# Moving the pooled v product to the head of three FFN slots, and the transposes onto other banks first

## The chip, the cores and the metric

The kernel runs on one core of a Trainium2 chip. The metric is the device time of one execution in microseconds, median of several runs. The TensorE clock in the page of the profile was granted in full for nearly the whole span.

Engines are called as the profile calls them: PE is TensorE, PEld its weight loads, ACT is ScalarE, DVE is VectorE, POOL is GpSimd.

## The reference

```python
# q, k, v: (8, 8, 576, 64); factor 4; scale = 1/8
q_d, k_d, v_d = mean over 4 neighbouring positions of q, k, v        # 144 positions
out_up    = repeat(softmax(scale * q_d @ k_d.T) @ v_d, 4)            # pooled attention
out_local = softmax(scale * q @ k.T where |i - j| < 4) @ v           # band attention
x   = (out_up + out_local) as 4608 tokens x 512
out = (relu(x @ w_gate) * (x @ w_val)) @ w_out                       # 512 -> 1536 -> 512
```

## The kernel before

The attention is worked off in 32 head pairs, `hp`. Four are done first (`emit_fill`); after that the program goes through "slots". Slot `s` holds a quarter of the FFN work of one chunk of 512 tokens, and between its parts the attention work of head pair `s + 4`, so that PE always has matmuls. Everything is scheduled by hand: on each engine the instructions run in the order in which the program emits them.

PSUM is one tile of eight banks, and `pair(i)` is banks 2i and 2i+1. The parts that matter, in slots 1 to 3:

| name in this text | line before / after | what it is | banks |
|---|---|---|---|
| denominators | L363, L372 / L367, L376 | column sums of the exponentials of the last head pair | 4, 5 |
| numerators | L382, L391 / L386, L395 | v times the exponentials | 2, 3 |
| projections | L483 / L487 | 4 matmuls for gate, 4 for value; three such pairs a slot | 0-1, 2-3, 6-7 |
| scores | L279, L290 / L283, L294 | q by k of this head pair | 4 to 7 |
| pooled v | L263 / L267 | 6 matmuls that sum v over 4 positions, and an ACT copy | 5, then 1 |
| transposes | L226 / L228 | q and k of the next head pair, 24 matmuls | 4, 0, 1 |

```python
def emit_qkT_pe(hp, b0, b1):
    ...                                         # cut
    blocks = list(range(2 * NB))                # 12 blocks, 4 to a bank
    if hp == 0:
        blocks = blocks[NB:] + blocks[:NB]
    for n in blocks:
        lo = 120 * (n % 4)
        bank = b0 if n < 4 else b1 + n // 4 - 1
        for hh in range(2):
            nc.tensor.matmul(out=ps[64 * hh : 64 * hh + 64, bank, lo : lo + 120],
                lhsT=sv[:, n // NB, hh, n % NB, :], rhs=eyesum_sb, start=True, stop=True)
    ...                                         # cut: views of the outputs
    act, dve = nc.scalar.copy, nc.vector.tensor_copy
    ...                                         # cut: the plan for hp == 0
    plan = ((0, 1, act), (0, 0, act), (1, 1, dve), (2, 1, dve), (2, 0, dve), (1, 0, act))
    for i, pooled, copy in plan:                # (bank index, pooled part?, engine)
        ...                                     # cut: copy of a bank's pooled or full part

def emit_vd(hp, bank):                          # pooled v
    t = vw[hp % NL][:, :, 0:64].rearrange("p (h j) d -> p j h d", h=2)
    o = ps[:, bank, 0:256].rearrange("p (c h d) -> p c h d", c=2, h=2)
    for c in range(2):
        for sig in range(3):
            nc.tensor.matmul(out=o[:, c, :, :], lhsT=pool_sb[0:WK, sig, :],
                rhs=t[:, 3 * c + sig, :, :], start=(sig == 0), stop=(sig == 2))
    nc.scalar.copy(out=vd[hp % 3].rearrange("p c (x d) -> p c x d", x=3)[:, :, 0:3:2, :], in_=o[0:72])

def emit_s2t(hp, between):
    ...                                         # cut: denominators into banks 4, 5
    ...                                         # cut: numerators into banks 2, 3
    r, x = rden[r2], xn[r2]
    nc.scalar.activation(out=r, in_=ps[:, 4:6, 0:360], func=AF.Ln)
    between()                                   # the gate of the previous projections
    nc.scalar.activation(out=r, in_=r, func=AF.Exp, scale=-1.0)
    nc.vector.tensor_tensor(out=x, in0=ps[:, 2:4, 0:360], in1=r, op=ALU.mult)
    emit_xsum(hp)

def emit_h(c, jj, pp, parts=...):               # projections into pair(pp)
    ...                                         # cut: the matmuls
    def gate():
        nc.scalar.activation(out=r1, in_=h1, func=AF.Relu)
        nc.vector.tensor_tensor(out=gt, in0=r1, in1=h2, op=ALU.mult)
    return gate

def emit_slot(s, gate):
    ...                                         # cut: loads, and slot 0
    if s <= 5:
        if s == 5:
            emit_pool(hp)
        emit_s2t(hp - 1, gate)
    ...                                         # cut: slots over 4
    if s == 4:
        emit_y(c - 1, s % 4, 1)
    else:
        emit_h(c, jj, 0)()
    emit_s1(hp, 4)                              # scores
    if s == 4:
        emit_h(c, jj, 0)()
    emit_h(c, jj + 1, 1)()
    emit_vd(hp, 5)
    if hp + 1 < NTP:
        emit_qkT_pe(hp + 1, 4, 0)
    return emit_h(c, jj + 2, 3)                 # its gate runs inside the next slot's emit_s2t
```

The softmax here doesn't subtract the row's maximum and nothing guards it: scores larger than these inputs give would overflow.

Of the kernel before, what the change touches and what calls it, by code (L numbers as in the profile page):

```python
# [57 lines left out]
def kernel(  # L58
# [25 lines left out]
    NTP = 9  # L84
# [122 lines left out]
    def emit_pool(hp):  # L207
        with nc.allow_low_precision(reason="4:1 pooling sum"):
            nc.vector.tensor_reduce(
                out=qkd[hp % 2].rearrange("p i t -> p (i t)"),  # L210
                in_=qkT[hp % 4][:, 0 : 2 * S].rearrange("p (t f) -> p t f", f=4),
                axis=AX.X,
                op=ALU.add,
            )

    def emit_qkT_pe(hp, b0, b1):
        r, r4, r2 = hp % NL, hp % 4, hp % 2
        sv = qk16[r].rearrange("p i (h j d) -> p i h j d", h=2, d=64)
        blocks = list(range(2 * NB))
        if hp == 0:  # L220
            blocks = blocks[NB:] + blocks[:NB]
        for n in blocks:
            lo = 120 * (n % 4)
            bank = b0 if n < 4 else b1 + n // 4 - 1
            for hh in range(2):
                nc.tensor.matmul(  # L226
                    out=ps[64 * hh : 64 * hh + 64, bank, lo : lo + 120],
                    lhsT=sv[:, n // NB, hh, n % NB, :],  # L228
                    rhs=eyesum_sb,
                    start=True,  # L230
                    stop=True,
                )
        big = qkT[r4][:, 0 : 2 * S].rearrange("p (b n t) -> p b n t", b=3, n=4)
        sml = qkd[r2].rearrange("p i t -> p (i t)").rearrange("p (b n t) -> p b n t", b=3, n=4)
        act, dve = nc.scalar.copy, nc.vector.tensor_copy
        if hp == 0:
            plan = ((2, 1, act), (2, 0, act), (1, 1, dve), (1, 0, dve), (0, 1, act), (0, 0, dve))
        else:
            plan = ((0, 1, act), (0, 0, act), (1, 1, dve), (2, 1, dve), (2, 0, dve), (1, 0, act))
        for i, pooled, copy in plan:  # L240
            bank = b0 if i == 0 else b1 + i - 1
            t = ps[:, bank, 0:480].rearrange("p (n t) -> p n t", n=4)
            if pooled:
                copy(out=sml[:, i], in_=t[:, :, 96:120])
            else:
                copy(out=big[:, i], in_=t[:, :, 0:96])

    def emit_vd_pool(hp):
        t, m, o = v4[hp % NV4], v2[hp % 2], vd[hp % 3]
        nc.gpsimd.tensor_tensor(out=m, in0=t[:, :, 0:128], in1=t[:, :, 128:256], op=ALU.add)  # L250
        nc.gpsimd.tensor_tensor(  # L251
            out=o.rearrange("p c (x d) -> p x c d", x=3)[:, 0:3:2, :, :],
            in0=m[:, :, 0:64].rearrange("p (h c) d -> p h c d", h=2),
            in1=m[:, :, 64:128].rearrange("p (h c) d -> p h c d", h=2),
            op=ALU.add,
        )

    def emit_vd(hp, bank):
# [4 lines that stand above are left out]
                nc.tensor.matmul(  # L263
                    out=o[:, c, :, :],
                    lhsT=pool_sb[0:WK, sig, :],
                    rhs=t[:, 3 * c + sig, :, :],
                    start=(sig == 0),  # L267
                    stop=(sig == 2),
                )
        nc.scalar.copy(  # L270
            out=vd[hp % 3].rearrange("p c (x d) -> p c x d", x=3)[:, :, 0:3:2, :], in_=o[0:72]
        )
# [85 lines left out]
    def emit_s2t(hp, between):  # L358
        r2 = hp % 2
        e, d = ee[r2], ed[r2]  # L360
        for g in range(2):
            for hh in range(2):
                nc.tensor.matmul(  # L363
                    out=ps[64 * hh : 64 * hh + 64, 4 + g, 0:288],
                    lhsT=ones_sb[0:WK, 0:64],
                    rhs=e[:, hh, 288 * g : 288 * g + 288],
                    start=True,  # L367
                    stop=True,
                )
            for c in range(2):  # L370
                for hh in range(2):
                    nc.tensor.matmul(  # L372
                        out=ps[64 * hh : 64 * hh + 64, 4 + g, 288:360],
                        lhsT=ones_sb[0:72, 64:128],
                        rhs=d[:, hh, c * SD + 72 * g : c * SD + 72 * g + 72],
                        start=(c == 0),  # L376
                        stop=(c == 1),
                    )
        for g in range(2):
            for j in range(3):  # L380
                for hh in range(2):
                    nc.tensor.matmul(  # L382
                        out=ps[64 * hh : 64 * hh + 64, 2 + g, NQ * j : NQ * j + NQ],
                        lhsT=vw[hp % NL][:, NB * hh + 3 * g + j, 0:64],
                        rhs=e[:, hh, 288 * g + NQ * j : 288 * g + NQ * j + NQ],
                        start=True,  # L386
                        stop=True,
                    )
            for c in range(2):
                for hh in range(2):  # L390
                    nc.tensor.matmul(  # L391
                        out=ps[64 * hh : 64 * hh + 64, 2 + g, 288:360],
                        lhsT=vd[hp % 3][:, c, 128 * hh : 128 * hh + 64],
                        rhs=d[:, hh, c * SD + 72 * g : c * SD + 72 * g + 72],
                        start=(c == 0),  # L395
                        stop=(c == 1),
                    )
        r, x = rden[r2], xn[r2]
        nc.scalar.activation(out=r, in_=ps[:, 4:6, 0:360], func=AF.Ln)  # L399
        between()  # L400
# [4 lines that stand above are left out]
    def emit_xsum(hp):  # L405
        b, kk, x = hp // NPB, hp % NPB, xn[hp % 2]
        nc.vector.tensor_tensor(  # L407
            out=xT[:, kk, b * S : (b + 1) * S].rearrange("p (c t f) -> p c t f", c=2, f=4),
            in0=x[:, :, 0:288].rearrange("p c (t f) -> p c t f", f=4),
            in1=_sap(x, (0, 128), 288, [[360, 2], [1, 72], [0, 4]]),  # L410
            op=ALU.add,
        )
# [184 lines left out]
    def emit_slot(s, gate):  # L597
        c, jj, hp = s // 4, 3 * (s % 4), s + LEAD
        if NVP <= hp + 1 < NP:
            emit_vd_pool(hp + 1)  # L600
        emit_in(hp + 4)
        if NTP <= hp + 3 < NP:
            emit_qkT(hp + 3)
        if s == 0:
            emit_qkT_pe(hp, 2, 3)
            emit_h_mm(c, jj, 3, 1, range(3))
            emit_h_mm(c, jj, 3, 0, range(1))
            emit_x_pe(hp - 1, 0)
            emit_h(c, jj, 3, ((0, range(1, 4)), (1, range(3, 4))))()
            emit_s1(hp, 2)  # L610
            emit_h(c, jj + 1, 0)()
            emit_vd(hp, 6)
            emit_qkT_pe(hp + 1, 2, 3)
            return emit_h(c, jj + 2, 3)
        if s <= 5:
            if s == 5:
                emit_pool(hp)
            emit_s2t(hp - 1, gate)
        elif gate:
            gate()  # L620
        if s > 4:
            if hp < NP:
                emit_y(c - 1, s % 4, 1 if s == 5 else 2, 6 if s == 5 else 2, lambda: emit_s1(hp, 4))
            else:
                emit_y(c - 1, s % 4, 2)
            if hp < NVP:
                emit_vd(hp, 3)
            if hp + 1 < NP:
                emit_pool(hp + 1)
            emit_h(c, jj, 0)()  # L630
            if hp < NP:
                emit_s2w(hp)
            emit_h(c, jj + 1, 1)()
            gate = emit_h(c, jj + 2, 0)
            if hp < NP:
                gate()
                emit_xsum(hp)
                return None
# [5 lines that stand above are left out]
        emit_s1(hp, 4)  # L644
        if s == 4:
            emit_h(c, jj, 0)()
        emit_h(c, jj + 1, 1)()
        emit_vd(hp, 5)
        if hp + 1 < NTP:
            emit_qkT_pe(hp + 1, 4, 0)  # L650
        return emit_h(c, jj + 2, 3)

    with tc.manual_schedule(engines={ET.PE, ET.DVE, ET.Activation, ET.SP, ET.Pool}):
# [49 lines left out]
```

## Time and profile before

| | before |
|---|---|
| time, median of the first 3 runs | 357.59 us (357.54 to 358.28) |
| span of the profiled run | 356.6 us |
| PE busy | 97% of the span |
| slots 1, 2 and 3 on PE | 8.29 us each |
| PE wait inside each of them | 0.26 us |

The first lines are from the page of the kernel before: the busy time of each engine, and the shares of the chain of work that ended last.

```profile
PE 347.2 (97%) x2851; PEld 177.8 (50%) x2851; DVE 227.0 (64%) x344; ACT 211.5 (59%) x358; POOL 189.0 (53%) x233
...
PE 90%; DVE 4%; ACT 3%; DMA 1%; issue 1%; DVEq 0%; POOLq 0%
```

The kernel is bound by PE. Time can only come from fewer matmuls or from the few places where PE stands still. Those are in the list of waits of PE (waiting line, what it waited for, total us, times, longest); these three lines lie in slots 1 to 3 and in slot 5:

```profile
PE ps L424 <- DVE ee_103 L302: 0.7, 1, 0.7
...
PE ps L483 <- DVE xn_114 L402: 0.5, 2, 0.3
PE ps L483 <- DVE xn_115 L402: 0.3, 1, 0.3
```

Next is slot 1 on PE, from the timeline (start, duration, what; several equal matmuls on one line; in brackets the idle time before and what ended it). A duration reaches to the end of the last result, so it overlaps the next line's start: read start to start.

```profile
31.90 1.03 PE L483 MATMUL ps<-xT,wv_sb 128*128 128x512 f16 x4
32.86 0.31 PE L363 MATMUL ps<-ee_102,ones_sb 112*64 112x288 f16 x2
...
34.63 1.03 PE L483 MATMUL ps<-xT,wv_sb 128*128 128x512 f16 x4
35.59 0.26 PE L279 MATMUL ps<-qkd_101 64*72 64x144 f16 x2
...
36.42 1.02 PE L483 MATMUL ps<-xT,wg_sb 128*128 128x512 f16 x4 [0.26 <-DVE xn_114 L402]
37.28 1.03 PE L483 MATMUL ps<-xT,wv_sb 128*128 128x512 f16 x4
38.14 0.50 PE L263 MATMUL ps<-vw_94,cst_sb 112*128 112x128 f16 x6
38.57 0.82 PE L226 MATMUL ps<-cst_sb,qk_6_81 96*64 96x120 f16 x24
...
41.15 0.31 PE L363 MATMUL ps<-ee_103,ones_sb 112*64 112x288 f16 x2
```

From 32.86 to 41.15 are 8.29 us. Only one line has a bracket. Pooled v at 38.14 starts as soon as the value projections let it (four matmuls of 0.216 us after 37.28), and has no wait. Six matmuls of 0.056 us end at about 38.48; the transposes start 0.09 us later, and the same gap stands before the denominators and before the scores, with no bracket.

The wait at 36.42 ends a chain on ACT and DVE. Here are ACT's lines from its timeline:

```profile
33.47 0.77 ACT L399 ACTIVATE rden_112<-ps 128x720 f32<-128x720 f32 x1 [1.70 <-PE ps L372]
34.14 0.59 ACT L498 ACTIVATE r_752<-ps 128x512 f16<-128x512 f32 x1
34.62 0.81 ACT L401 ACTIVATE rden_112<-rden_112 128x720 f32<-128x720 f32 x1
```

And DVE's line that PE waits for:

```profile
35.46 0.91 DVE L402 TENSOR_TENSOR xn_114<-ps,rden_112 128x720 f16<-128x720 f32 x1
```

The denominators end, then come the logarithm, the gate relu of the previous projections, the exponential, and the product, which reads banks 2 and 3. The second projections want to write those banks.

### The profile page before, as it was taken

What the parts mean: (1) busy time and instruction counts of PE and PEld (TensorE: products, weight loads), DVE (VectorE), ACT (ScalarE), POOL (GpSimd) and SP (SyncE); (2) the same over time, 40 slices, a digit from 0 to 9 for tenths busy, and PEclk for the clock granted to TensorE, in tenths of its full rate; (3) what the DMA queues carried; (4) which work ended last, traced back from release to release, by engine and by line L of the source; (5) the groups of instructions that cost most, each with busy time, mean ns of one, the idle gap of its engine ahead of it and who ended that gap; (6) DMA issues with size and microseconds to landing.
All of it is one profiled execution on the core that took longest, in us unless ns stands there. A gap on an engine that the chain in (4) does not pass through costs nothing.

```text
span 356.6 us, 7224 instructions
## 1 busy us (share of the span) xinstructions
PE 347.2 (97%) x2851; PEld 177.8 (50%) x2851; DVE 227.0 (64%) x344; ACT 211.5 (59%) x358; POOL 189.0 (53%) x233
## 2 busy tenths in 40 slices
PE   6999999999999999999999999999999999999995
PEld 2665555545554555555555555555544444444443
DVE  5894666686776777777787888877765523222220
ACT  3767775666667776666666666666667532322321
POOL 8986558899999777777778877711000000000000
PEclk9999999999999999999999999999999999999999
DMA  9999999999999999999999999930000100000022
GB/s 149 168 171 188 180 196 163 165 196 169 182 154 158 148 130 131 131 130 131 131 134 134 122 120 137 133 83 30 31 28 20 45 30 29 31 29 29 31 59 89
DMA packets 167170, 40.25 MB, mean 113 GB/s; under 512 B 149888, under 2 KB 162656, under 8 KB 167136
## 3 DMA queue, kind: packets, MB, share of 16 engines
q0 software_dynamic: 132960, 22.93, 83.7%
q1 hardware_dynamic: 28832, 7.53, 14.6%
q10 hardware_dynamic: 5344, 9.34, 7.6%
q8 instruction: 22, 0.36, 0.4%
q14 instruction: 12, 0.10, 0.1%
HBM read 46.45 MB, written 9.44 MB: 157 GB/s over the span
## 4 chain that ended last, share of the span: by engine, by line
PE 90%; DVE 4%; ACT 3%; DMA 1%; issue 1%; DVEq 0%; POOLq 0%
PE ps L483 51%; PE ps L510 25%; PE ps L424 3%; PE ps L226 2%; PE ps L290 2%; PE ps L279 2%; PE ps L432 2%; DMA qk_0_75<-in_k_dram 1%; DVE xn_114 L402 1%; PE ps L540 1%; DVE xT L407 1%; ACT rden_112 L399 1%; ACT rden_112 L401 1%; PE ps L363 1%; PE ps L263 0%
## 5 line engine op out<-in xcount | busy, mean ns | idle before, releaser
L483 PE MATMUL ps<-xT,wg_sb 128*128 128x512 f16 x432 | 111.3, 380 | 0.9 <-DVE xn_114 L402 0.5
L483 PE MATMUL ps<-xT,wv_sb 128*128 128x512 f16 x432 | 111.0, 379 | 0.0
L510 PE MATMUL ps<-wo_sb,gT 128*128 128x512 f16 x420 | 100.1, 380 | 0.0
L483 PEld LDWEIGHTS <-wv_sb 128*128 128x128 f16 x432 | 42.2, 98 | 50.7
L483 PEld LDWEIGHTS <-wg_sb 128*128 128x128 f16 x432 | 39.8, 97 | 44.4 <-issue 0.7
L510 PEld LDWEIGHTS <-gT 128*128 128x128 f16 x420 | 39.1, 98 | 45.5
L518 ACT COPY y_sb<-ps 128x512 f32<-128x512 f32 x35 | 20.5, 587 | 46.9 <-PE ps L510 46.9
L448 DVE TENSOR_TENSOR xn_115<-ps,rden_113 64x720 f16<-64x720 f32 x24 | 21.7, 905 | 21.7 <-ACT rden_113 L445 21.3
L448 DVE TENSOR_TENSOR xn_114<-ps,rden_112 64x720 f16<-64x720 f32 x22 | 19.9, 905 | 21.1 <-ACT rden_112 L445 20.8
L299 ACT ACTIVATE ee_102<-ps 112x576 f16<-112x576 f32 x32 | 19.0, 647 | 13.5 <-PE ps L290 12.9
L299 ACT ACTIVATE ee_103<-ps 112x576 f16<-112x576 f32 x32 | 19.0, 647 | 12.7 <-PE ps L290 12.5
L442 ACT ACTIVATE rden_113<-ps 64x720 f32<-64x720 f32 x24 | 18.3, 764 | 7.0 <-PE ps L432 6.7
L302 DVE TENSOR_TENSOR ee_102<-ee_102,cst_sb 112x576 f16<-112x576 f16 x32 | 20.0, 659 | 1.3 <-ACT ee_102 L299 1.1
L442 ACT ACTIVATE rden_112<-ps 64x720 f32<-64x720 f32 x22 | 16.8, 764 | 6.0 <-PE ps L432 5.7
L302 DVE TENSOR_TENSOR ee_103<-ee_103,cst_sb 112x576 f16<-112x576 f16 x32 | 19.4, 645 | 0.0
L407 DVE TENSOR_TENSOR xT<-xn_114 128x576 f16<-128x576 f16 x14 | 13.3, 948 | 0.1
L579 PE MATMUL ps<-zero_sb 128*128 128x512 f16 x29 | 9.7, 446 | 1.3 <-DVE zero_sb L131 1.3
L407 DVE TENSOR_TENSOR xT<-xn_115 128x576 f16<-128x576 f16 x14 | 10.9, 778 | 0.1
L308 ACT ACTIVATE ed_105<-ps 72x576 f16<-72x576 f32 x16 | 10.3, 642 | 0.0
L308 ACT ACTIVATE ed_104<-ps 72x576 f16<-72x576 f32 x16 | 10.3, 642 | 0.0
L445 ACT ACTIVATE rden_113<-rden_113 128x720 f32<-128x720 f32 x12 | 9.6, 804 | 0.4
L251 POOL TENSOR_TENSOR vd_106<-v_0_87 72x256 f16<-72x256 f32 x4 | 2.9, 721 | 12.2 <-PE ps L432 12.2
(464 smaller groups left out, 599.9 us busy)
## 6 DMA issues: line engine op xcount, KB each, us to landing
out_dram<-y_sb ACTq DMA_DIRECT2D x34, 256.0 KB, 3.9
wg_sb<-in_moe_w_gate_dram POOLq DMA_DIRECT2D x4, 384.0 KB, 9.6
wv_sb<-in_moe_w_val_dram POOLq DMA_DIRECT2D x4, 384.0 KB, 10.5
wo_sb<-in_moe_w_out_dram POOLq DMA_DIRECT2D x4, 384.0 KB, 12.1
vw_90<-in_v_dram POOLq DMA_DIRECT2D x5, 168.0 KB, 6.2
vw_91<-in_v_dram POOLq DMA_DIRECT2D x5, 168.0 KB, 6.0
vw_92<-in_v_dram POOLq DMA_DIRECT2D x5, 168.0 KB, 5.9
v_4_86<-in_v_dram POOLq DMA_DIRECT2D x5, 144.0 KB, 6.5
```

The lines of the kernel that those rows point to most:

```text
L299: nc.scalar.activation(out=o, in_=ps[0:WK, p0 + 2 * g : p0 + 2 * g + 2, 0:288], func=AF.Exp, scale=scale)
L302: nc.vector.tensor_tensor(out=o, in0=o, in1=_sap(masks_sb, (0, WK), 288 * g, [[0, 2], [1, 288]]), op=ALU.mult,)
L308: nc.scalar.activation(out=ed[r2][:, :, 0 : 2 * SD].rearrange("p h (c t) -> p c h t", c=2), in_=ps[0:72, p0 : p0 + 4, 288:432].rearrange(" ...
L407: nc.vector.tensor_tensor(out=xT[:, kk, b * S : (b + 1) * S].rearrange("p (c t f) -> p c t f", c=2, f=4), in0=x[:, :, 0:288].rearrange("p ...
L424: nc.tensor.matmul(out=ps[:, bank, NQ * j : NQ * j + NQ], lhsT=vflat[:, v0 : v0 + 128], rhs=e[:, hh, lo : lo + NQ], start=True, stop=True,)
L442: nc.scalar.activation(out=r[lo : lo + 64], in_=ps[de : de + 64, 4 + 2 * hh : 6 + 2 * hh, 0:360], func=AF.Ln)
L445: nc.scalar.activation(out=r, in_=r, func=AF.Exp, scale=-1.0)
L448: nc.vector.tensor_tensor(out=x[lo : lo + 64], in0=ps[lo : lo + 64, 4 + 2 * hh : 6 + 2 * hh, 0:360], in1=r[lo : lo + 64], op=ALU.mult,)
L483: nc.tensor.matmul(out=pair(pp)[:, which, :], lhsT=w[:, kk, bass.ts(jj, 128)], rhs=xT[:, kk, c * TCH : (c + 1) * TCH], start=(kk == 0), st ...
L510: nc.tensor.matmul(out=y_ps, lhsT=gts[c, jj][:, bass.ts(ty, 128)], rhs=wo_sb[:, jj, :], start=(jj == 0), stop=(jj == NJJ - 1),)
L518: nc.scalar.copy(out=y_sb, in_=y_ps)
L579: nc.tensor.matmul(out=ps[:, 7, :], lhsT=zero_sb[:, 0:128], rhs=zero_sb[:, 128:640], start=True, stop=True)
```

## The change

Its intent: pooled v leaves its place between the second projections and the transposes and goes to the slot's head, where bank 1 is free; the transposes then follow the projections directly and fill the banks 0 and 1, free earliest, before bank 4. The ScalarE and VectorE copies are re-dealt to follow the new order of the banks.

In the diff, `s < 4` means slots 1 to 3, since slot 0 returns before these lines.

```diff
-    def emit_qkT_pe(hp, b0, b1):
+    def emit_qkT_pe(hp, b0, b1, b0_last=False):
...
         if hp == 0:
             blocks = blocks[NB:] + blocks[:NB]
+        elif b0_last:
+            blocks = blocks[4:] + blocks[:4]
...
+        elif b0_last:
+            plan = ((1, 1, act), (1, 0, act), (2, 1, dve), (2, 0, dve), (0, 1, dve), (0, 0, act))
...
         if s <= 5:
             if s == 5:
                 emit_pool(hp)
+            elif s < 4:
+                emit_vd(hp, 1)
             emit_s2t(hp - 1, gate)
...
         emit_h(c, jj + 1, 1)()
-        emit_vd(hp, 5)
-        if hp + 1 < NTP:
-            emit_qkT_pe(hp + 1, 4, 0)
+        if s == 4:
+            emit_vd(hp, 5)
+        else:
+            emit_qkT_pe(hp + 1, 4, 0, True)
         return emit_h(c, jj + 2, 3)
```

## The prediction

> **What bounds the kernel now.** TensorE: the page gives PE 347.2 us of a 356.6 us span (97%) at full clock, and the chain that ended last is 90% PE. The change touches only FFN slots 1 to 3. Each takes 8.29 us on the PE timeline, from its first denominator matmul to the next slot's (32.86, 41.15, 49.45, 57.74).
>
> Such a slot holds three pairs of projections, 24 matmuls of 0.216 us, 5.18 us; the previous head pair's denominators and numerators, about 0.9; scores, about 0.5; pooled v, 6 matmuls, 0.34; transposes, 24 matmuls, 0.75; and two losses. The first is about 0.09 us at each step from full-width to half-array matmuls: projections to denominators (41.06 to 41.15), projections to scores, pooled v to transposes (38.48 to 38.57). The Trainium skill, "TensorEngine Tiling (Array Packing)", Key Properties, says that changing the tiling mode drains TensorE; this trace agrees, with that 0.09 us. The second is one real wait: 0.26 us before the second projection pair, for the VectorE product that empties banks 2 and 3 (list of waits: 0.8 us in all).
>
> **What the change removes, adds, moves.** Nothing is added or removed. Three times, six pooled-v matmuls (0.34 us) and their ScalarE copy (0.37) move from before the transposes to before the denominators, and the transposes start with banks 0 and 1; each engine keeps the same number and sizes of copies.
>
> - Old place: bank 5 was free (the last exponential ends 37.73) when pooled v started (38.14), so no PE wait is removed. Transposes likewise: banks 4 and 1 are free at 37.73 and 37.76, and they would now start about 38.23. The bank order saves nothing.
> - Mode changes: projections to pooled v cost none. The drain before the transposes and the one before the denominators both stay. Net zero.
> - The 0.26 us wait is a race of the chain denominators, logarithm (0.77), gate relu, exponential (0.8), product (0.91) against the PE work from denominators to second projections (numerators, one pair, scores). Both start at the denominators; the moved work lies before both. The wait stays.
> - The pooled-v copy must finish before the logarithm: it ends about 0.9 us after the slot's head, the denominators at about 1.0. It just fits; if not, each slot loses about 0.1.
> - Bank 1 at the slot's head: the transposes' copies are over about 0.8 us before. The v tile for slot 1 was requested at 18.5 us and landed in under 9, before its new use at 32.8.
>
> **On the critical path:** the moved PE work, before and after, at the same cost. I expect 8.29 us a slot, within 0.1.
>
> **Predicted time 357.6 us**, 8 in 10 between 357.1 and 358.2. Even all three waits gone would be 0.8 us, 0.2%. Chances: faster by over 2% 0.005, within 2% 0.99, slower by over 2% 0.005.
>
> **Right if** the profile after shows slots of 8.29 us, the same three waits of 0.26 us on the product, no new PE wait at pooled v or transposes, drains of about 0.09 us before denominators and transposes, the logarithm starting right after the denominators. **Wrong if** PE waits for bank 1 at the slot's head; or the pooled-v copy holds up the logarithm (wait 0.3 to 0.4); or the 0.26 us wait shrinks, so that some step of that chain is not tied to the denominators as I read it; or mode changes cost differently in the new order.

## The result, and the profile after

| | before | after |
|---|---|---|
| time, median of 6 runs each | 358.25 us (357.54 to 359.42) | 357.82 us (357.57 to 358.03) |
| ratio | | 0.9986, 95% interval 0.9967 to 1.0005 |
| span of the profiled run | 356.6 us | 356.0 us |
| last line ahead of slot 1's head to the denominators of slot 4 | 31.90 to 57.74 = 25.84 us | 31.82 to 57.66 = 25.84 us |

A ratio is the mean time of one kernel's runs over that of the other's of the same rounds, so it is not quite the ratio of the medians. Here its interval includes 1. In the profile the three slots together take the same time to the last digit shown.

The page after:

```profile
PE 346.9 (97%) x2851; PEld 177.8 (50%) x2851; DVE 226.4 (64%) x344; ACT 211.9 (60%) x358; POOL 188.7 (53%) x233
...
PE 90%; DVE 4%; ACT 3%; DMA 1%; issue 1%; DVEq 0%; POOLq 0%
```

The list of waits of PE after (the lines that answer to those of before):

```profile
PE ps L487 <- DVE xn L406: 0.8, 3, 0.3
...
PE ps L428 <- DVE ee L306: 0.4, 1, 0.4
```

Slot 1 on PE, after:

```profile
31.82 1.03 PE L487 MATMUL ps<-xT,wv_sb 128*128 128x512 f16 x4
32.68 0.50 PE L267 MATMUL ps<-vw,cst_sb 112*128 112x128 f16 x6
33.11 0.31 PE L367 MATMUL ps<-ee,ones_sb 112*64 112x288 f16 x2
...
35.84 0.25 PE L283 MATMUL ps<-qkd 64*72 64x144 f16 x2
...
36.67 1.02 PE L487 MATMUL ps<-xT,wg_sb 128*128 128x512 f16 x4 [0.26 <-DVE xn L406]
37.53 1.03 PE L487 MATMUL ps<-xT,wv_sb 128*128 128x512 f16 x4
38.49 0.82 PE L228 MATMUL ps<-cst_sb,qk 96*64 96x120 f16 x24
...
40.98 0.50 PE L267 MATMUL ps<-vw,cst_sb 112*128 112x128 f16 x6
41.41 0.31 PE L367 MATMUL ps<-ee,ones_sb 112*64 112x288 f16 x2
```

Pooled v has moved to 32.68 and everything from the denominators to the second projections comes 0.33 us later after the slot's head, which is the length of pooled v (six matmuls of 0.056 us). From scores to second projections it is 0.83 us in both (35.59 to 36.42, 35.84 to 36.67), and the wait of 0.26 us is there. The gap of 0.09 us now stands between projections and transposes (37.53 and four times 0.216 is 38.39, and the transposes start at 38.49), and pooled v has one to the denominators behind it, as it had one to the transposes before.

ACT in the same slot, after, with the copy of pooled v ahead of the logarithm:

```profile
33.22 0.37 ACT L274 CAST vd<-ps 72x256 f16<-72x256 f32 x1 [1.53 <-PE ps L267]
33.73 0.77 ACT L403 ACTIVATE rden<-ps 128x720 f32<-128x720 f32 x1
34.39 0.59 ACT L502 ACTIVATE r<-ps 128x512 f16<-128x512 f32 x1
```

The copy is over at 33.59 and the logarithm starts at 33.73, 0.05 us after the last denominator's end (33.68).

The two spans still differ by 0.6 us. The first transposes start at 6.47 before and 6.37 after, as the first load of k lands: 0.1 us. At slot 4 the difference is 0.08 us, after slot 5's numerators it is 0.57 us, and it stays so to the end (the last matmul group ends at 353.0 and 352.4). Slot 5 has the same program in both. What differs there is DVE. Before:

```profile
70.99 2.33 DVE L407 TENSOR_TENSOR xT<-xn_114 128x576 f16<-128x576 f16 x1
73.24 1.34 DVE L302 TENSOR_TENSOR ee_103<-ee_103,cst_sb 112x576 f16<-112x576 f16 x2
```

After:

```profile
70.91 0.76 DVE L411 TENSOR_TENSOR xT<-xn 128x576 f16<-128x576 f16 x1
71.59 2.43 DVE L306 TENSOR_TENSOR ee<-ee,cst_sb 112x576 f16<-112x576 f16 x2
```

An operation that takes 0.76 us alone takes 2.33 us in one trace, and in the other it is the next one that is stretched. In both, GpSimd runs its own sum just then; from the timeline of POOL before:

```profile
71.53 1.16 POOL L250 TENSOR_TENSOR v_0_87<-v_0_82 72x512 f32<-72x512 f16 x1
72.77 1.13 POOL L251 TENSOR_TENSOR vd_107<-v_0_87 72x256 f16<-72x256 f32 x1
```

The Trainium skill, "SBUF — State Buffer", Who interferes with whom, says that a VectorE instruction with two inputs in SBUF contends with a GpSimd instruction that reads SBUF, for a pair of ports that it calls an exclusive lock. Both DVE operations have two SBUF inputs, and the traces agree that they contend, with 0.76 against 2.33 us; they do not tell a blocked operation from a slowed one. Which of the DVE operations is met, and so how long PE waits behind it (0.7 us before, 0.4 after), hangs on a small shift between the two engines: GpSimd's first sum (71.53 before, 71.62 after) starts 0.54 us after DVE's sum into `xT` before, and 0.71 us after it in the changed kernel. This was read from traces; no run was made to take the GpSimd sum away. The other profiles bear it out, though. In 12 of the 14 kept here, the sum into `xT` or the masks behind it, or both, are stretched, and GpSimd's sum starts before the masks are over. In the other two it starts 0.33 and 0.45 us after the masks are over, and neither is stretched.

### The profile page after: what moved, and what is told of

Same layout as the page of the kernel before. It is cut to its first block, busy times and chain, and to the rows that moved or that the text cites. A ratio compares the mean times of both kernels' runs of the same rounds, so it can differ in the third digit from the quotient of the medians.

```text
span 356.0 us, 7222 instructions
## 1 busy us (share of the span) xinstructions
PE 346.9 (97%) x2851; PEld 177.8 (50%) x2851; DVE 226.4 (64%) x344; ACT 211.9 (60%) x358; POOL 188.7 (53%) x233
## 4 chain that ended last, share of the span: by engine, by line
PE 90%; DVE 4%; ACT 3%; DMA 1%; issue 1%; DVEq 0%; POOLq 0%
PE ps L487 51%; PE ps L514 25%; PE ps L428 3%; PE ps L228 2%; PE ps L294 2%; PE ps L283 2%; PE ps L436 2%; DMA qk<-in_k_dram 1%; DVE xn L406 1%; ACT rden L403 1%; DVE xo L355 1%; ACT rden L405 1%; PE ps L544 1%; DVE ee L306 1%; ACT r L502 1%
## 5 line engine op out<-in xcount | busy, mean ns | idle before, releaser
L504 DVE TENSOR_TENSOR gT<-r,ps 128x512 f16<-128x512 f16 x108 | 71.9, 684 | 67.3 <-PE ps L487 45.5
L502 ACT ACTIVATE r<-ps 128x512 f16<-128x512 f32 x108 | 64.0, 593 | 33.5 <-PE ps L487 30.8
L452 DVE TENSOR_TENSOR xn<-ps,rden 64x720 f16<-64x720 f32 x46 | 41.6, 905 | 42.5 <-ACT rden L449 41.8
L303 ACT ACTIVATE ee<-ps 112x576 f16<-112x576 f32 x64 | 38.1, 647 | 26.2 <-PE ps L294 25.4
L446 ACT ACTIVATE rden<-ps 64x720 f32<-64x720 f32 x46 | 35.2, 764 | 12.8 <-PE ps L436 12.2
L306 DVE TENSOR_TENSOR ee<-ee,cst_sb 112x576 f16<-112x576 f16 x64 | 40.9, 677 | 1.3 <-ACT ee L303 1.1
L174 POOL DMA_DIRECT2D qk<-in_q_dram x46 | 34.2, 745 | 4.3 <-DMA wo_sb<-in_moe_w_out_dram 2.8
L174 POOL DMA_DIRECT2D qk<-in_k_dram x46 | 33.3, 729 | 0.5 <-DMA vw<-in_v_dram 0.3
L209 DVE TENSOR_REDUCE qkd<-qkT 128x288 f16<-128x1152 f16 x23 | 30.9, 1342 | 0.0
L254 POOL TENSOR_TENSOR v<-v 72x512 f32<-72x512 f16 x23 | 30.2, 1314 | 0.3
## 6 DMA issues: line engine op xcount, KB each, us to landing
wv_sb<-in_moe_w_val_dram POOLq DMA_DIRECT2D x4, 384.0 KB, 10.5
```

The costliest lines, as they stand in the source:

```text
L174: nc.gpsimd.dma_start(dv[:, :, hh, :], _dap(src, off + hh * S * D, [[D, 96], [NQ * D, NB], [1, D]]),)
L209: nc.vector.tensor_reduce(out=qkd[hp % 2].rearrange("p i t -> p (i t)"), in_=qkT[hp % 4][:, 0 : 2 * S].rearrange("p (t f) -> p t f", f=4), ...
L254: nc.gpsimd.tensor_tensor(out=m, in0=t[:, :, 0:128], in1=t[:, :, 128:256], op=ALU.add)
L303: nc.scalar.activation(out=o, in_=ps[0:WK, p0 + 2 * g : p0 + 2 * g + 2, 0:288], func=AF.Exp, scale=scale)
L306: nc.vector.tensor_tensor(out=o, in0=o, in1=_sap(masks_sb, (0, WK), 288 * g, [[0, 2], [1, 288]]), op=ALU.mult,)
L446: nc.scalar.activation(out=r[lo : lo + 64], in_=ps[de : de + 64, 4 + 2 * hh : 6 + 2 * hh, 0:360], func=AF.Ln)
```

## The experiments

The theory: pooled v was not held up and held nothing up at its old place, and its new place costs the same; the 0.26 us wait is a race between the chain from denominators to product and PE's work from denominators to second projections, and the moved work lies outside that race. Rivals: the 0.14% of the first runs is a gain of the change; one part gains and the other loses; small PE work hides in slack wherever it stands; the 0.26 us are no wait but a fixed cost of the step.

Twelve runs were made, two of them repeats, all with right results. Line numbers move a little with the edits. For some of them `emit_vd` was given arguments: `times` (how often the matmuls are issued), `copies` (how often the copy) and `eng` (the engine of the copy).

### The changed kernel again

No edit.

> The changed kernel again. Theory (the change moves work between two places of equal cost): 0 to 0.1% from the kernel before, slots 1 to 3 of 8.29 us each with a 0.26 us wait in each; any difference of the spans lies outside slots 1 to 3, at the first k load or at VectorE in slot 5. Rival (the 0.14% of the first runs is a gain of the change): 0.14% faster again, and the gain shows between 32 and 58 us on the timeline.

Measured: 358.07 us median, against 357.57 for the kernel before on that chip, ratio 1.0008 (0.9993 to 1.0022). Slots 1 and 2 took 8.30 and 8.29 us, three waits, 0.8 us in all. The gain of 0.14% did not come back: it was spread, not the change. This profile had a start of its own, with a granted clock of 0.89 from 5 to 10 us and 0.77 from 10 to 15, and its slot 1 came 1.4 us later than in the first profile of the same kernel. In it, the three warm-up matmuls that fell into the stretch of half clock took 1.49 us, while three at full clock had taken 0.82.

### Each part alone

Only pooled v moved, the transposes in their old order and with their old copies:

```diff
-            emit_qkT_pe(hp + 1, 4, 0, True)
+            emit_qkT_pe(hp + 1, 4, 0)
```

> Pooled v at the slot's head in bank 1, transposes in the old bank order and with the old copies. Theory: as before, slots 8.29 us, wait 0.26 us, time within 0.2% of before. Rival (the new bank order is needed to make the move pay or not hurt): a PE wait at the transposes for bank 4, or slots longer than 8.3 us.

Only the transposes reordered, pooled v back at its old place in bank 5:

```diff
-            elif s < 4:
-                emit_vd(hp, 1)
...
-        if s == 4:
-            emit_vd(hp, 5)
-        else:
+        emit_vd(hp, 5)
+        if s < 4:
             emit_qkT_pe(hp + 1, 4, 0, True)
```

> Pooled v at its old place in bank 5, transposes in the new bank order with the new copies. Theory: as before, slots 8.29 us, wait 0.26 us, within 0.2%. Rival (one part gains and the other loses, and the sum is zero): this or the other part alone differs by 0.1 us or more a slot.

Measured: the move alone, ratio 1.0018 (0.9998 to 1.0037), slots of 8.29 and 8.30 us, waits as before (and a slow start, like the one told next). The order alone, ratio 1.0033 (1.0014 to 1.0052), with slots of 8.29, 8.30 and 8.29 us and the same waits. By the time the second rival seemed right, by the slots it was wrong. The profile of that slow kernel shows the loss before slot 1, in instructions that the change does not touch; this is its first group of transposes:

```profile
6.32 1.41 PE L228 MATMUL ps<-cst_sb,qk 96*64 96x120 f16 x24 [0.61 <-DMA qk<-in_k_dram]
```

In the profile of before, the same 24 matmuls took 0.82 us (at 6.47), and the three warm-up matmuls behind them took 0.82 against 1.46 us. From the first transposes to slot 1's denominators it was 27.23 us (6.32 to 33.55) against 26.39 before (6.47 to 32.86), so 0.84 us were lost there.

> The kernel with only the transposes' order changed, once more, because its first runs were 0.33% slower while its slots 1 to 3 read 8.29 us each. Theory (the first runs fell on slow starts: in their profile the first transposes took 1.41 us instead of 0.82, about 1 us lost before slot 1): this time within 0.2% of before, slots 8.29 us. Rival (the new order with pooled v at its old place really costs 1 us): 0.3% slower again.

Measured: 357.96 us against 357.93, ratio 1.0002 (0.9989 to 1.0015), slots of 8.30, 8.29 and 8.29 us, and this start:

```profile
6.30 0.82 PE L228 MATMUL ps<-cst_sb,qk 96*64 96x120 f16 x24 [0.75 <-DMA qk<-in_k_dram]
```

The 0.33% was not the order. That the first profile of this kernel had a slow start is shown, and that start was a matter of the clock: the trace's record of a full clock begins only at 10.5 us (at 4.6 us in the profile of before), and until then its warm-up matmuls start 0.43 us apart, where the others start 0.22 us apart. That its other three runs had such a start too is likely, but they have no trace. Neither part does anything by itself.

### Work doubled, at the head and inside the race

Two kernels issue the six pooled-v matmuls twice. One does it at the slot's head:

```diff
-                emit_vd(hp, 1)
+                emit_vd(hp, 1, times=2)      # six matmuls twice, then one copy
```

> The changed kernel with the six pooled-v matmuls issued twice at the slot's head (same result). Theory: work at the head lies ahead of both sides of the race for banks 2 and 3 and is paid in full: slots 8.29 + 0.34 = 8.63 us, wait still 0.26 us, +1.0 us in all. Rival (the slot has slack that hides small PE work wherever it stands): slots under 8.45 us, wait shorter than 0.26 us.

The other repeats them after the numerators, before the first projections, into bank 1, unread:

```diff
             emit_s2t(hp - 1, gate)
+            if s < 4 and s > 0:
+                emit_vd(hp, 1, copies=0)     # six matmuls, no copy
```

> The changed kernel with the six pooled-v matmuls issued a second time, into bank 1, after the numerators (the second result is overwritten unread; the output stays right). Theory: this work stands between the denominators and the second projections, so it fills the 0.26 us wait: no wait left, slots 8.29 + 0.34 - 0.26 = 8.37 us, +0.25 us in all. Rival (the 0.26 us are a fixed cost of the step from scores to projections and no wait): slots 8.63 us, as with the work doubled at the head.

At the head: slots of 8.63 us (33.11 to 41.74 to 50.37), the three waits of 0.26 us still there, ratio 1.0032 (1.0013 to 1.0051), which is 1.1 us. The work was paid in full, as the theory had it.

```profile
32.35 0.83 PE L268 MATMUL ps<-vw,cst_sb 112*128 112x128 f16 x12
...
36.67 1.02 PE L489 MATMUL ps<-xT,wg_sb 128*128 128x512 f16 x4 [0.26 <-DVE xn L408]
```

Inside the race: no wait on the product in the list, slots of 8.32 and 8.31 us, ratio 1.0002 (0.9979 to 1.0025).

```profile
33.83 0.51 PE L268 MATMUL ps<-vw,cst_sb 112*128 112x128 f16 x6
...
36.27 0.29 PE L296 MATMUL ps<-qkT 64*128 64x96 f16 x6
36.49 1.04 PE L489 MATMUL ps<-xT,wg_sb 128*128 128x512 f16 x4
```

The second projections at 36.49 have no bracket. The same six matmuls cost 0.34 us a slot in one place and 0.03 in the other. The first refutes the slack, the second the fixed cost. The expectation was missed by 0.05 us a slot, to the good side; the next two runs miss by the same, and the reason is told below.

### Pooled v itself inside the race

Pooled v moves from the slot's head to the place that the last run found, with its copy on DVE, which is idle there for about 3 us:

```diff
-            elif s < 4:
-                emit_vd(hp, 1)
-            emit_s2t(hp - 1, gate)
+            emit_s2t(hp - 1, gate, hp if s < 4 else None)
...
-    def emit_s2t(hp, between):
+    def emit_s2t(hp, between, fill=None):
...                                          # after the numerators
+        if fill is not None:
+            emit_vd(fill, 1, eng=nc.vector.tensor_copy)
```

> Pooled v moved from the slot's head to between the numerators and the first projections (bank 1), copied by VectorE, which is idle there. Theory: its 0.34 us fill the wait: none left, slots 8.29 - 0.26 = 8.03 us, 0.8 us (0.2%) faster than before. Rival (the position of pooled v does not matter): slots 8.29 us.

Measured: slots of 7.98 us, no wait on the product, 357.13 us against 357.72, ratio 0.9978 (0.9955 to 1.0000).

```profile
33.71 0.51 PE L268 MATMUL ps<-vw,cst_sb 112*128 112x128 f16 x6
...
36.38 1.04 PE L491 MATMUL ps<-xT,wg_sb 128*128 128x512 f16 x4
```

So by the slots the position does matter, if it lies between the denominators and the second projections.

### The other side of the race

The gate relu goes first on ACT, so that it leaves the chain:

```diff
             elif s < 4:
+                gate()
                 emit_vd(hp, 1)
-            emit_s2t(hp - 1, gate)
+            emit_s2t(hp - 1, gate if s >= 4 else (lambda: None))
```

> The changed kernel with the gate relu of the previous projections put ahead of the pooled-v copy and the logarithm in ScalarE's order, in slots 1 to 3. Theory: the relu (0.49 us) leaves the chain from denominators to the VectorE product, which then ends before the scores do: no wait, slots 8.03 us, 0.8 us (0.2%) faster than before. Rival (relu or copy now hold up the logarithm, or banks 6 and 7 set the time): slots 8.1 us or more, or a new PE wait.

Measured: slots of 7.98 us, 356.95 us against 357.72, ratio 0.9970 (0.9949 to 0.9990). ACT's timeline shows the new order:

```profile
31.90 0.60 ACT L502 ACTIVATE r<-ps 128x512 f16<-128x512 f32 x1 [0.33 <-PE ps L487]
33.10 0.37 ACT L274 CAST vd<-ps 72x256 f16<-72x256 f32 x1 [0.60 <-PE ps L267]
33.60 0.77 ACT L403 ACTIVATE rden<-ps 128x720 f32<-128x720 f32 x1
34.41 0.80 ACT L405 ACTIVATE rden<-rden 128x720 f32<-128x720 f32 x1
```

The relu uses time in which ACT had been idle, logarithm and exponential follow each other, and on PE the second projections follow the scores without a bracket:

```profile
35.72 0.25 PE L283 MATMUL ps<-qkd 64*72 64x144 f16 x2
...
36.22 1.04 PE L487 MATMUL ps<-xT,wg_sb 128*128 128x512 f16 x4
```

From scores to projections it is now 0.50 us, where it was 0.83. The wait had cost 0.33 us there, while the profile gave it as 0.26. The Trainium skill, "Perfetto Trace Analysis", Tensor Engine Instruction, says that the end of a matmul in the profile is estimated. The idle time counts from that end, but a matmul that waits for nothing starts before it: the last scores here start at 36.00 and last 0.29 us, to 36.29, and the projections start at 36.22. Those 0.07 us are the difference. About 0.02 us come back in the first projections after a wait (1.02 in place of 1.04 us), which leaves the 0.31 us a slot that the slots show (8.29 to 7.98).

The same edit in the kernel before, with pooled v at its old place:

```diff
-            emit_s2t(hp - 1, gate)
+            if s < 4:
+                gate()
+            emit_s2t(hp - 1, gate if s >= 4 else (lambda: None))
```

> The kernel before (pooled v and transposes at their old places) with the gate relu ahead of the logarithm in slots 1 to 3. Theory (the place of pooled v is neutral in this too, and the relu was all of the wait): slots 7.98 us, no wait, 0.9 us (0.26%) faster than before, the same as the changed kernel with the same edit. Rival (the relu may only go first because pooled v stands at the head and gives it time): the logarithm starts late, slots 8.05 us or more.

Measured: slots 1 to 3 of 7.98, 7.98 and 7.99 us with no wait in them; ratio 0.9984 (0.9968 to 1.0001). Its profile had the slow start again (the first transposes 1.41 us, span 356.3) and a wait of 0.4 us in slot 5, so its time is not compared closely with the run above. By the slots, the place of pooled v is neutral here as well.

### How tight the copy is

The ACT copy of pooled v, done twice:

```diff
-                emit_vd(hp, 1)
+                emit_vd(hp, 1, copies=2)
```

> The changed kernel with the ScalarE copy of pooled v done twice (same result). Theory: the first copy has about 0.14 us to spare before the logarithm, so a second one of 0.33 us holds it up by about 0.2 us and the wait grows to about 0.46 us: slots 8.49 us, +0.6 us in all. Rival (the copy is off the chain): slots 8.29 us.

Measured: slots of 8.44 and 8.45 us, ratio 1.0011 (0.9985 to 1.0037), and the wait grown:

```profile
36.61 1.02 PE L489 MATMUL ps<-xT,wg_sb 128*128 128x512 f16 x4 [0.41 <-DVE xn L408]
```

The mechanism is as expected, the size 0.15 us a slot and not 0.20. One by one in the trace, the copies start at 33.00 and 33.40 and the logarithm at 33.67: the second copy cost 0.40 us and not 0.33, and the logarithm started 0.27 us after it, before its recorded end. An estimate from these numbers: with one copy ACT is free for the logarithm 0.27 us after 33.22, at 33.49, while the logarithm started at 33.73. So the copy had about 0.24 us to spare and not 0.14.

### The gate relu first in slots 1 to 5, in both kernels

```diff
-            elif s < 4:
-                emit_vd(hp, 1)
-            emit_s2t(hp - 1, gate)
+            gate()
+            if 0 < s < 4:
+                emit_vd(hp, 1)
+            emit_s2t(hp - 1, lambda: None)
```

> The changed kernel with the gate relu first in slots 1 to 5. Theory: 0.9 us from slots 1 to 3; and in slot 5 the wait of the numerators for the VectorE mask product, 0 to 0.7 us from run to run, is gone too, because its chain also begins with the logarithm: 0.9 to 1.6 us (0.25 to 0.45%) faster than before. Rival (slot 5's wait is made by VectorE and GpSimd blocking one another): it stays in some profile.

In the kernel before, with pooled v at its old place:

```diff
-            emit_s2t(hp - 1, gate)
+            gate()
+            emit_s2t(hp - 1, lambda: None)
```

> The kernel before with the gate relu first in slots 1 to 5. Theory: the same time as the changed kernel with this edit, within 0.1%, slots 1 to 3 of 7.98 us, no wait in slots 1 to 5. Rival: the two differ by 0.2% or more, and the place of pooled v matters once the wait is gone.

Measured: with the change 356.67 us, ratio 0.9969 (0.9952 to 0.9986); without it 356.75 us, ratio 0.9973 (0.9950 to 0.9996); the kernel before 357.93 on that chip. Slots of 7.98 us in both. The two ratios differ by 0.04%, far less than their intervals are wide, so no effect of pooled v's place shows here either. Nor does it show that the slots 4 and 5 add anything: with slots 1 to 3 alone the ratios were 0.9970 and 0.9984. The rival about slot 5 holds: the run with the change still had a wait of 0.2 us there, with the mask products of DVE at 2.46 us while the GpSimd sum ran beside them from 70.94. (The masks began at 69.97 and would have ended at about 70.79, a little before that, so the start that the profile gives for GpSimd is only rough.) In the other run the masks came before the sum, which began at 71.44, were not stretched, and PE did not wait:

```profile
69.49 0.76 DVE L407 TENSOR_TENSOR xT<-xn 128x576 f16<-128x576 f16 x1
70.17 0.82 DVE L302 TENSOR_TENSOR ee<-ee,cst_sb 112x576 f16<-112x576 f16 x2
```

Either of these two versions beats the kernel before, by about 1.0 to 1.1 us or 0.3%. That is clear of the noise but small. The changed kernel was not run beside them.

## Why the prediction was right or wrong

The time was right: 357.6 us predicted, 357.82 measured, and no difference from before. That alone says little, because it is what "nothing changes" predicts (the kernel before had a median of 357.59 in its first runs); the slots and waits are the test. Point by point:

- "no PE wait is removed": right. Neither pooled v nor the transposes had a bracket before, and each part alone left the slots at 8.29 us.
- "Mode changes ... Net zero": right. The gap of 0.09 us moved with its neighbours and their number stayed.
- "Both start at the denominators; the moved work lies before both. The wait stays": right, and tested from four sides. Work doubled before the denominators was paid in full with the wait unchanged; work doubled after them filled the wait; pooled v put after them gained 0.31 us a slot; and with the relu out of the chain the wait was gone.
- The pooled-v copy "just fits": right. It ends 0.91 us after the head and the denominators 1.00 us; the spare time is about 0.24 us by the doubled copy.
- Bank 1 at the head was free in time: right. The last VectorE copy out of it (the large one at 39.44 in slot 1, 0.55 us) was over 1.0 us before 40.98, against 0.8 predicted.
- "Even all three waits gone would be 0.8 us": the mechanism right, the term too small. The sum took the profile's 0.26 us as the cost of a wait. Its cost is 0.31 us a slot, 0.93 us in all.
- Not foreseen: the re-dealt copies made ACT wait 0.63 us for DVE at its last copy out of bank 4 (40.18 in slot 1). It is over at 40.66, 0.75 us before the denominators want that bank, so it costs nothing.

## What to carry to other kernels

To know what moving a piece of work can bring, find the wait on the bounding engine, follow its chain back to where it and the bounding engine part, and see on which side of that point the work lies. Work before that point, or after the wait is over, is paid in full wherever it stands; work between that point and the wait fills the wait; and an operation that only shares a queue with the chain can be taken out of it. When the whole effect is below half a percent, compare the stretch that the change touches in the profiles, because starts and chance collisions elsewhere move the total as much.

## What the Trainium skill lacked or had wrong

- "TensorEngine Tiling (Array Packing)", Key Properties, says that a change of tiling mode drains TensorE but gives no size for it. Here it was about 0.09 us at each step from full-width to half-array matmuls, wherever that step was put. The steps back cost about as much: in the trace of before, the transposes go in pairs 0.053 us apart, the last pair starts at 39.17, and the projections follow at 39.32, 0.10 us later than a next pair would.
- "Perfetto Trace Analysis", Tensor Engine Instruction, says that a matmul's end is estimated, but not what this does to waits. Here a wait shown as 0.26 us cost 0.33 us at its place and 0.31 us in the slot.
- "SBUF — State Buffer", Who interferes with whom, agrees with the runs, but gives no time for this pair of operations: a VectorE sum of 128x576 f16 with two SBUF inputs went from 0.76 to 2.33 us when it met a GpSimd sum.
- "TensorE: Matmul & The Clock Gate", What's actually happening, says that the warm-up of the clock varies from run to run. The runs agree: the record of a full clock begins between 4.2 and 5.9 us in eleven of the 14 profiles and between 10.2 and 10.5 us in three, and in these three the first 24 transposes took 1.41 us, not 0.82. (The view of the profile by windows counts the time before that record as full clock, so it shows 1.00 between 5 and 10 us in both.) The page puts the ramp under 1% of a span; the slow start cost 0.84 us, 0.2%. That agrees, but it is nearly as much as the largest effect studied here.
